# Identity products in TensorE's gaps until the first FFN product, and V sorting of batch 0 through three PSUM banks

## The chip, the cores and the metric

The kernel runs on one core of a Trainium2 chip. The metric is device microseconds of one execution; the runs shown are given by their median. The profile is of one further execution, recorded by the hardware profiler. Times within it count from the start of its span.

The core has a matrix engine (TensorE, "PE" in the profile, with weight loads as "PEld"), VectorE ("DVE"), ScalarE ("ACT"), GpSimd ("POOL") and SyncE ("SP"), each working through its own list of instructions in order. Matrix products land in PSUM, which the kernel uses as eight banks of 512 f32 columns. Transfers are issued by GpSimd and SyncE and run on 16 DMA engines.

## The reference

Two stages in a row. First block-sorted attention for 4 batches, 8 heads, 768 positions in 8 blocks of 96, head size 64:

```
P = sort_net                        # [4, 8, 8, 8]
five times: P = exp(P - rowmax); P /= rowsum; P /= columnsum
k_sorted = einsum('bhij,bhjcd->bhicd', P, k_blocks)      # blocks mixed by P
v_sorted = einsum('bhij,bhjcd->bhicd', P, v_blocks)
scores   = q_block @ k_sorted_block.T / 8                 # block by block, 96 x 96
attn     = softmax(scores)
x        = attn @ v_sorted_block                          # [3072 tokens, 512]
```

Then a feed-forward network (FFN): `h = x @ w_in` (512 to 2048), `g = max(h, 0) + alpha * min(h, 0)`, `out = g @ w_out` (2048 to 512), in f32.

## The kernel before, in words

**Groups and stages.** Attention works on 32 groups g (batch g // 8, block g % 8), each with all 8 heads. Before a batch's groups, its K and V are sorted. K sorting of a batch is six units (`prep_k`, products of line 542), V sorting eight units (`prep_v`, products of line 585). Each unit is 16 small products into one PSUM bank and one copy out of it (line 372, `copy`), by ScalarE or VectorE. V is first copied into another layout (`conv_v`, tile VD from VST). The matrices of the sorting weights, BDK, come from the Sinkhorn steps on VectorE and ScalarE (`sinkhorn`, `spread`).

**A group of batch 0** is: scores (line 625, `s1`), row maxima on VectorE (line 631), scores once more transposed and with the maxima taken off by identity products (lines 646 and 637, `s2`), exp on ScalarE (line 669, tile Es), product with sorted V (line 678, `o`), reciprocal and scaling on VectorE (lines 683 and 686, tile xq), transpose on TensorE (line 701), and copy to xT. A group of a later batch takes its maxima off inside the exp (line 658) and is transposed by DMA (lines 663 and 694, tiles ET and xT). Groups 0 and 1 run side by side: group 0 uses psS and psO, group 1 uses psH for scores and psYP for its output.

**The FFN** takes chunks of 2 or 4 groups of tokens. `ffn1` is four products of line 723 into a bank, a ReLU of the negated bank on ScalarE (line 733, tile t) and a combination on VectorE that reads the bank again (line 736, tile hT). `ffn2` is four parts of four products each (line 762) and a copy out.

**PSUM banks.** psS, psO, psH and psYP have two banks each. `BANK_O` are the banks of psO, `BANK_H` those of psH, `BANK_Y` is bank 0 of psYP and `BANK_P` its bank 1. While `ffn1` works on the first two groups it also uses `BANK_P`; the sorting of batch 1 goes through `BANK_P` alone. V sorting of batch 0 goes through both banks of psO, `BANK_P` and `BANK_Y` in turn (line 795).

**The order of the work** isn't written out. Every piece is an operation in a graph (`_Graph`) with an estimated duration, a priority and the tiles that it reads and writes. `schedule` plays the graph through with these estimates and puts each engine's operations in order; for operations that may run on ScalarE or VectorE it also picks the engine. `search` does so 1500 times with priorities changed at random (a fixed seed) and keeps the order with the lowest estimated end. The result is a fixed list for each engine, with semaphore waits. A change in the graph changes the search, and so the order of the whole kernel.

**Filling.** After the search, `fill` goes through TensorE's list. Where the estimates leave a gap inside one of the given spans of time, it puts a block of identity products into it that nobody reads: as many as take 0.9 of the gap. They write `BANK_Y`, 512 columns each (`warm`, line 877). There are two spans: from 5 us to the first V sorting unit that uses `BANK_Y`, and from the first `ffn1` product to the first `ffn2` product.

**Loads.** GpSimd issues all loads of q, k, v and the weights: q, k and v of batch 0, the four parts of w_in, the two of w_out, k of batch 1 (line 419), q of batch 1 in eight parts (line 401), then v of batch 1 and k and v of batch 2 (line 419). `ffn1` needs w_in, `ffn2` needs the halves of w_out, K sorting of batch 1 needs KS and its V layout copies need VST.

Of the kernel before, what the change touches and what calls it, by code (L numbers as in the profile page):

```python
# [8 lines left out]
AP = bass.AP  # L9
# [26 lines left out]
def t_pe(*mms):  # L36
    return sum(max(n, m, 64) / 2.4 + 4 for n, m in mms)


def t_act(n):  # L40
    return 170 + n / 1.2
# [19 lines left out]
class _Graph:  # L61
# [138 lines left out]
            op.prio = p  # L200
        return self.schedule()

    def fill(self, make, unit, first, spans):

        out, last = [], self.ops[first].end + 300
        for op in self.order["pe"]:
            for lo, hi in spans:
                begin = max(last, lo)
                n = int((op.start - begin) * 0.9 / unit)
                if op.start <= hi and n > 0:  # L210
                    x = _Op("pe", lambda e, n=n: make(e, n), n * unit, 0.0, None, len(self.ops))
                    x.start, x.end = begin, begin + n * unit
                    x.deps.add(first)
                    self.ops.append(x)
                    out.append(x)
            out.append(op)
            last = max(last, op.end)
        for pos, op in enumerate(out):
            op.pos = pos
        self.order["pe"] = out  # L220
# [69 lines left out]
def bass_sinkhorn_attn__then__act_prelu_kernel(  # L290
# [11 lines left out]
    G = _Graph()  # L302
    sems = {e: es.enter_context(nc.semaphore("s_" + e)) for e in ENGS}

    def dma_sem(name):
        return [es.enter_context(nc.semaphore("d_" + name)), 0]
# [7 lines left out]
    PE, ACT, DVE, POOL, SYNC = ("pe",), ("act",), ("dve",), ("pool",), ("sync",)  # L314
# [251 lines left out]
                                               AP(KT[0], 0, [[ld, 128], [bk, 32], [1, 16]])), 900,  # L566
                  r=[("KT", 0, 0), ("KT", 0, 1)], w=["KTpad"], prio=prio + 1)

    first_y = []

    def conv_v(b, u, prio):
        o = AP(VD, 8 * u * 64, [[4096, 128], [64, 8], [1, 48]])
        i = AP(VST[b % 2], 8 * u, [[3072, 128], [1, 8], [64, 48]])
# [3 lines left out]
    def prep_v(b, u, prio, bank=BANK_P):  # L577
        t, off, row, keys = bank
        n = b % 2

        def f(e):
            inst = None
            for dd in range(8):
                for th in range(2):
                    inst = e.matmul(AP(t, th * 64 * row + off + dd * 64, [[row, 64], [1, 64]]),  # L585
                                    AP(VD, (8 * u + dd) * 64, [[4096, 128], [1, 64]]),
                                    AP(BDK, b * 128 + th, [[512, 128], [2, 64]]))
            return inst
        op = G.add(PE, f, 374, r=[("VD", u), "VD0", ("BDK", b)], w=keys, prio=prio)
        if keys == ["psY"]:  # L590
            first_y.append(op)
        o = AP(VS[n], 8 * u, [[64 * 65, 112], [65, 64], [1, 8]])
        i = AP(t, off, [[row, 112], [1, 64], [64, 8]])
        G.add(EITHER, lambda e: copy(e, o, i), {"act": 685, "dve": 690}, r=keys + [("VS1", n)], w=[("VS", n, u)],
              prio=prio)

    d_e = [dma_sem("e%d" % n) for n in range(NE)]
    d_x = [dma_sem("x%d" % n) for n in range(NE)]

    def attention(g, prio):  # L600
# [53 lines left out]
        if far:  # L654
            def ex(e):
                inst = None
                for p in range(8):
                    inst = e.activation(AP(Esb[me], p * 128, [[1024, 96], [64, 2], [1, 48]]),  # L658
                                        AP(psX, (p // 4) * 512 + (p % 4) * 96, [[1024, 96], [48, 2], [1, 48]]),
                                        ACTF.Exp, bias=nf[m][:, p:p + 1])  # L660
                return inst
            G.add(ACT, ex, 8 * 245, r=banks_s + [("Epad", me), ("nf", m)], w=[("Esb", me)], prio=prio)
            G.add(SYNC, lambda e: e.dma_start_transpose(
                AP(ET[me], 0, [[800, 128], [96, 8], [1, 96]]), AP(Esb[me], 0, [[1024, 96], [1, 1024]])),
                5000 if g < 18 else 3100, r=[("Esb", me)], w=[("ET", me), ("turned", g)], prio=prio, dma=(d_e[me], 0))
        else:
            G.add(PE, s2, 700, r=kt_keys + qt_keys + [("nm", m), "identb"],
                  w=banks_s, prio=ps_)
            G.add(ACT, lambda e: e.activation(
                AP(Es0[m], 0, [[800, nk], [384, 2], [1, 384]]),  # L670
                AP(psX, 0, [[1024, nk], [512, 2], [1, 384]]),
                ACTF.Exp), t_act(768), r=banks_s, w=[("Es0", m)], prio=ps_)

        def o(e):
            inst = None
# [3 lines left out]
                                    AP(ET[me] if far else Es0[m], pos(h4, hp) * 96, [[800, nk], [1, 128]]),  # L679
                                    AP(VS[n], ((hp * 4 + h4) * 8 + i) * 65, [[64 * 65, nk], [1, 65]]))  # L680
            return inst
        G.add(PE, o, t_pe(*[(65, 65)] * 8), r=vs_keys + ([("ET", me), ("ETtail", me)] if far else [("Es0", m), ("Etail", m)]), w=banks_o, prio=prio)
        G.add(DVE, lambda e: e.reciprocal(AP(rec[m], 0, [[8, 96], [4, 2], [1, 4]]),  # L683
                                          AP(psZ, 64, [[1024, 96], [512, 2], [68, 4]])), 200,
              r=banks_o, w=[("rec", m)], prio=prio)
# [106 lines left out]
    for u in range(8):  # L792
        conv_v(0, u, -45.5)
    for u in range(8):
        prep_v(0, u, -45, (BANK_O + [BANK_P, BANK_Y])[u % 4])
    for kt in range(KT_TILES):
        G.add(POOL, lambda e, kt=kt: e.dma_start(
            AP(w_in_bf, kt * DFF, [[KT_TILES * DFF, 128], [1, DFF]]),
# [72 lines left out]
    assert fp == len(ffn_plan)  # L871
    total = G.search(SEARCH)

    def warm(e, n):
        inst = None
        for _ in range(n):
            inst = e.matmul(psYP[:, 0, :], identb[:, :], AP(identb, 0, [[128, 128], [0, 4], [1, 128]]))  # L877
        return inst
    G.fill(warm, 215, ident_op, [(5000, first_y[0].start), (ffn_ops[0].start + 1, ffn_ops[1].start)])
    if __import__("os").environ.get("SCHED"):  # L880
        print("scheduled", total)
        for e in ENGS:
# [37 lines left out]
```

## Time and profile before

| | |
|---|---|
| runs shown | 253.9, 254.17, 256.3 us; median 254.17 |
| the profiled execution | 255.69 us, its span 254.0 us |
| TensorE busy | 235.3 us (93%) |
| VectorE, ScalarE, GpSimd busy | 171.5, 160.5, 38.5 us |
| identity products of line 877 | 34, 10.6 us |
| first FFN product | 27.61 us |
| first K and V sorting of batch 1 on TensorE | 42.03 and 52.09 us |

In the page's table of slices each digit is one fortieth of the span, 6.35 us, and gives the busy share in tenths; 9 is 90% or more. PEclk is the clock granted to TensorE in tenths of full speed. In the chain of work that ended last, the FFN products of lines 723 and 762 have 29% and 26 + 3% of the span. A timeline row gives start, duration, engine, line, operation, output and inputs, shape and count, and in brackets the idle time before it and what ended it.

### The profile page before, as it was taken

What the parts mean: (1) busy time and instruction counts of PE and PEld (TensorE: products, weight loads), DVE (VectorE), ACT (ScalarE), POOL (GpSimd) and SP (SyncE); (2) the same over time, 40 slices, a digit from 0 to 9 for tenths busy, and PEclk for the clock granted to TensorE, in tenths of its full rate; (3) what the DMA queues carried; (4) which work ended last, traced back from release to release, by engine and by line L of the source; (5) the groups of instructions that cost most, each with busy time, mean ns of one, the idle gap of its engine ahead of it and who ended that gap; (6) DMA issues with size and microseconds to landing.
All of it is one profiled execution on the core that took longest, in us unless ns stands there. A gap on an engine that the chain in (4) does not pass through costs nothing.

```text
span 254.0 us, 6423 instructions
## 1 busy us (share of the span) xinstructions
PE 235.3 (93%) x2679; PEld 140.7 (55%) x2679; DVE 171.5 (68%) x347; ACT 160.5 (63%) x429; POOL 38.5 (15%) x63
## 2 busy tenths in 40 slices
PE   4796899989997978989899999999999999999995
PEld 1455678657654544556555555555555555555554
DVE  5887668796856775977885666656667765645530
ACT  4475446598866765878866485766677457534531
POOL 8995000000360011037000000000000000000000
PEclk9999589999999999999999999999999999999999
DMA  5999999999999999999979345233234433311103
GB/s 102 211 211 203 181 215 166 216 188 187 101 159 106 172 162 143 220 146 183 94 158 149 67 115 130 50 90 85 71 70 122 80 66 88 90 58 40 43 5 122
DMA packets 75534, 32.17 MB, mean 127 GB/s; under 512 B 67808, under 2 KB 71152, under 8 KB 75504
## 3 DMA queue, kind: packets, MB, share of 16 engines
q0 software_dynamic: 23632, 13.63, 41.1%
q1 hardware_dynamic: 51872, 18.11, 38.7%
q8 instruction: 21, 0.34, 0.6%
q14 instruction: 9, 0.07, 0.1%
HBM read 27.28 MB, written 6.29 MB: 132 GB/s over the span
## 4 chain that ended last, share of the span: by engine, by line
PE 75%; DVE 12%; DMA 9%; ACT 2%; issue 1%
PE psH L723 29%; PE psYP L762 26%; DMA ET<-Esb 8%; PE psS L762 3%; PE psO L678 3%; PE psS L622 3%; PE psYP L585 3%; PE psYP L542 2%; DVE hT L736 2%; DVE VD L372 2%; DVE VS L372 1%; PE psYP L877 1%; PE psS L637 1%; DVE KT L372 1%; ACT Esb L658 1%
## 5 line engine op out<-in xcount | busy, mean ns | idle before, releaser
L736 DVE SCALAR_TENSOR_TENSOR hT<-t,omaT,psH 128x384 bf16<-128x384 f32 (+1 forms) x139 | 77.5, 572 | 39.7 <-ACT t L733 38.1
L723 PE MATMUL psH<-xT,w_in_bf 128*128 128x384 bf16 (+1 forms) x556 | 98.5, 314 | 1.6 <-DVE hT L736 1.3
L733 ACT ACTIVATE t<-psH 128x384 f32<-128x384 f32 (+1 forms) x139 | 62.8, 466 | 44.5 <-PE psH L723 41.4
L762 PE MATMUL psYP<-w_out_bf,hT 128*128 128x512 bf16 x336 | 83.9, 379 | 1.0 <-DVE hT L736 0.6
L723 PEld LDWEIGHTS psH<-xT,w_in_bf 128*128 128x128 bf16 x556 | 50.8, 99 | 35.0 <-DVE hT L736 7.8
L658 ACT ACTIVATE Esb<-psS,nf 96x96 bf16<-96x96 f32 x192 | 46.3, 345 | 2.1 <-DVE nf L631 2.1
L762 PEld LDWEIGHTS psYP<-w_out_bf,hT 128*128 128x128 bf16 x336 | 30.7, 98 | 29.7 <-DVE hT L736 0.7
L401 POOL DMA_DIRECT2D QN<-in_q_dram x24 | 20.0, 857 | 45.2 <-DMA QTz<-QN 44.5
L631 DVE TENSOR_REDUCE nf<-psS 96x8 f32<-96x768 f32 x24 | 22.7, 948 | 3.9 <-PE psS L622 3.9
L686 DVE TENSOR_TENSOR xq<-psO,rec 96x512 bf16<-96x512 f32 x31 | 21.3, 686 | 1.0
L372 ACT ACTIVATE VS<-psYP 112x512 bf16<-112x512 f32 x17 | 11.7, 689 | 6.3 <-PE psYP L585 6.2
L372 ACT ACTIVATE outstg<-psYP 128x512 f32<-128x512 f32 x15 | 9.0, 597 | 9.9 <-PE psYP L762 9.8
L585 PE MATMUL psYP<-BDK,VD 128*64 128x64 bf16 x448 | 12.4, 198 | 1.9 <-DVE hT L736 1.0
L683 DVE RECIPROCAL rec<-psO 96x8 f32<-96x8 f32 x31 | 6.2, 201 | 11.7 <-PE psO L678 11.7
L877 PE MATMUL psYP<-identb 128*128 128x512 bf16 x34 | 10.6, 451 | 3.4 <-ACT identb L372 3.4
L585 PEld LDWEIGHTS psYP<-BDK,VD 128*64 128x64 bf16 x448 | 9.3, 111 | 6.9 <-issue 1.8
L622 PEld LDWEIGHTS psS<-KT,QTz 128*96 128x96 bf16 x192 | 11.7, 124 | 2.5
L678 PEld LDWEIGHTS psO<-VS,ET 112*128 112x128 bf16 x192 | 8.6, 98 | 7.6 <-DMA ET<-Esb 4.4
L622 PE MATMUL psS<-KT,QTz 128*96 128x96 bf16 x192 | 12.7, 209 | 0.0
L678 PE MATMUL psO<-VS,ET 112*128 112x65 bf16 x192 | 9.9, 194 | 2.8 <-DMA ET<-Esb 2.6
L372 DVE COPY VD<-VST 128x384 bf16<-128x384 bf16 x20 | 10.5, 565 | 1.4 <-DMA VST<-in_v_dram 1.4
L372 ACT ACTIVATE KT<-psYP 128x512 bf16<-128x512 f32 x11 | 6.6, 600 | 6.7 <-PE psYP L542 6.5
(115 smaller groups left out, 174.6 us busy)
## 6 DMA issues: line engine op xcount, KB each, us to landing
out_dram<-outstg SPq DMA_DIRECT2D x23, 256.0 KB, 2.2
KS<-in_k_dram POOLq DMA_DIRECT2D x3, 768.0 KB, 33.4
VST<-in_v_dram POOLq DMA_DIRECT2D x3, 768.0 KB, 29.1
QN<-in_q_dram POOLq DMA_DIRECT2D x24, 96.0 KB, 5.9
w_in_bf<-in_moe_w_in_dram POOLq DMA_DIRECT2D x4, 512.0 KB, 17.7
w_out_bf<-in_moe_w_out_dram POOLq DMA_DIRECT2D x2, 1024.0 KB, 28.4
QS<-in_q_dram POOLq DMA_DIRECT2D x1, 768.0 KB, 6.6
VST<-in_v_dram POOLq DMA_DIRECT2D x4, 192.0 KB, 4.6
```

Source lines behind the costliest of these rows:

```text
L372: return e.activation(o, i, ACTF.Copy) if e is nc.scalar else e.tensor_copy(o, i)
L401: G.add(POOL, lambda e, h=h: e.dma_start(AP(QN, h * 128 + (h // 4) * 64, [[6144, 128], [1024, 6], [1, 64]]), AP(q.tensor, b * HB + h * S * ...
L585: inst = e.matmul(AP(t, th * 64 * row + off + dd * 64, [[row, 64], [1, 64]]), AP(VD, (8 * u + dd) * 64, [[4096, 128], [1, 64]]), AP(BDK, b ...
L622: inst = e.matmul(o, AP(QTz[n], hp * 3072 + h4 * 768 + i * 96, [[6144, 128], [1, 96]]), AP(KT[n], (h4 * 8 + i) * bk, [[ld, 128], [64, 2], ...
L631: G.add(DVE, lambda e: e.tensor_reduce(AP(nx, 0, [[8, 96], [4, 2], [1, 4]]), AP(psX, 0, [[1024, 96], [512, 2], [96, 4], [1, 96]]), AxisLis ...
L658: inst = e.activation(AP(Esb[me], p * 128, [[1024, 96], [64, 2], [1, 48]]), AP(psX, (p // 4) * 512 + (p % 4) * 96, [[1024, 96], [48, 2], [ ...
L678: inst = e.matmul(AP(psZ, hp * 512 + h4 * 68, [[1024, 128], [1, 65]]), AP(ET[me] if far else Es0[m], pos(h4, hp) * 96, [[800, nk], [1, 128]]),
L686: G.add(DVE, lambda e: e.tensor_tensor(out=AP(xq[me], 0, [[512, 96], [256, 2], [64, 4], [1, 64]]), in0=AP(psZ, 0, [[1024, 96], [512, 2], [ ...
L723: inst = e.matmul(AP(pt, poff, [[1024, 128], [1, n]]), AP(w_in_bf, kt * DFF + ft * 128, [[KT_TILES * DFF, 128], [1, 128]]), AP(xT, kt * XR ...
L733: G.add(ACT, lambda e: e.activation(AP(t1[tb], 0, [[384, 128], [1, n]]), AP(pt, poff, [[1024, 128], [1, n]]), ACTF.Relu, scale=-1.0), t_ac ...
L736: G.add(DVE, lambda e: e.scalar_tensor_tensor(out=AP(hT, ft * RING + tok % RING, [[FT_TILES * RING, 128], [1, n]]), in0=AP(t1[tb], 0, [[38 ...
L762: inst = e.matmul(AP(bank[0], bank[1], [[1024, 128], [1, n]]), AP(hT, ft * RING + tok % RING, [[FT_TILES * RING, 128], [1, 128]]), AP(w_ou ...
```

## The change

The spans given to `fill` now carry what a block of identity products must wait for and the bank that it writes. There are three: from 5 us to group 1's output product, into `BANK_Y`, after the identity matrix is made; from there to the first `ffn1` product, into the first bank of psH, after group 1's exp, the last reader of its scores there; and from there to the first `ffn2` product, into `BANK_Y` again. An identity product now has 256 columns with an estimate of 108 ns, in place of 512 and 215. So that `BANK_Y` is free of V sorting until group 1's output, the V sorting of batch 0 takes three banks in turn, both of psO and `BANK_P`.

```diff
@@ class _Graph
-    def fill(self, make, unit, first, spans):
-
-        out, last = [], self.ops[first].end + 300
+    def fill(self, make, unit, spans):
+
+        out, last = [], 0.0
         for op in self.order["pe"]:
-            for lo, hi in spans:
-                begin = max(last, lo)
+            for lo, hi, deps, bank in spans:
+                begin = max([last, lo] + [self.ops[d].end + 300 for d in deps])
                 n = int((op.start - begin) * 0.9 / unit)
                 if op.start <= hi and n > 0:
-                    x = _Op("pe", lambda e, n=n: make(e, n), n * unit, 0.0, None, len(self.ops))
+                    x = _Op("pe", lambda e, n=n, bank=bank: make(e, n, bank), n * unit, 0.0, None, len(self.ops))
                     x.start, x.end = begin, begin + n * unit
-                    x.deps.add(first)
+                    x.deps.update(deps)
                     self.ops.append(x)
                     out.append(x)
             out.append(op)
...
@@ prep_v
-        op = G.add(PE, f, 374, r=[("VD", u), "VD0", ("BDK", b)], w=keys, prio=prio)
-        if keys == ["psY"]:
-            first_y.append(op)
+        G.add(PE, f, 374, r=[("VD", u), "VD0", ("BDK", b)], w=keys, prio=prio)
...
@@ attention: group 1's exp and output product are noted
+            if g == 1:
+                warm_at["exp"] = op
...
+        if g == 1:
+            warm_at["out"] = op
...
     for u in range(8):
-        prep_v(0, u, -45, (BANK_O + [BANK_P, BANK_Y])[u % 4])
+        prep_v(0, u, -45, (BANK_O + [BANK_P])[u % 3])
...
-    def warm(e, n):
+    def warm(e, n, bank):
+        t, off, row, keys = bank
         inst = None
         for _ in range(n):
-            inst = e.matmul(psYP[:, 0, :], identb[:, :], AP(identb, 0, [[128, 128], [0, 4], [1, 128]]))
+            inst = e.matmul(AP(t, off, [[row, 128], [1, 256]]), identb[:, :], AP(identb, 0, [[128, 128], [0, 2], [1, 128]]))
         return inst
-    G.fill(warm, 215, ident_op, [(5000, first_y[0].start), (ffn_ops[0].start + 1, ffn_ops[1].start)])
+    out1, f1, f2 = warm_at["out"].start, ffn_ops[0].start, ffn_ops[1].start
+    G.fill(warm, 108, [(5000, out1, [ident_op], BANK_Y), (out1 + 1, f1, [warm_at["exp"].idx], BANK_H[0]),
+                       (f1 + 1, f2, [ident_op], BANK_Y)])
```

In the built order there are 87 identity products ahead of the first FFN product (29 of twice the width before) and 12 between the first FFN product and the first product of line 762 (5 before). Since the bank turn of V sorting enters the graph, the search gives another order, from the K sorting of batch 0 to the end of the kernel.

## The prediction

> **What bounds the kernel now.** I read the page's 40 slices first, then the clock by its own windows, then TensorE's timeline from 20 to 60 us, then when the loads land. In the slices TensorE (PE) is near full from 28 us on. The clock row has one dip, and the DMA row is full until slice 20 (127 us).
>
> ```profile
> PE   4796899989997978989899999999999999999995
> PEclk9999589999999999999999999999999999999999
> DMA  5999999999999999999979345233234433311103
> ```
>
> The dip, cut into stretches of 3.41 us (a row: stretch, its length, busy time and count of TensorE, granted clock, DMA share, GB/s):
>
> ```profile
> 19.83:23.24 3.41, 2.59 (x101) 1.00 1.07 215
> 23.24:26.65 3.41, 1.50 (x28) 1.00 1.03 156
> 26.65:30.06 3.41, 3.26 (x39) 0.50 1.20 194
> 30.06:33.47 3.41, 3.41 (x25) 0.50 1.24 207
> ...
> 9.60:13.00 3.40, 1.90 (x16) 1.00 0.99 204
> ```
>
> After a stretch that was 44% busy (1.50 of 3.41) the clock is halved for 6.82 us, though no single gap in that stretch exceeds 0.77 us. A stretch 56% busy (9.60 to 13.00) did not halve it. So the share of a stretch seems to decide, with the limit between 44 and 56%.
>
> What the dip costs: from the first FFN product (27.61 us) to 33.47 us TensorE did work that takes about 3.1 us at full clock (sums of the same groups in later rows: 0.66 for 8 FFN products of 192 columns, 0.28 + 0.36 for the second score pass, 0.65 for three identity products, and so on). It took 5.8 us, so 2.7 us are lost. Will the end get them? Two later places decide:
>
> ```profile
> 27.61 1.46 PE L723 MATMUL psH<-xT,w_in_bf 128*128 128x192 bf16 x8
> ...
> 42.03 0.44 PE L542 MATMUL psYP<-BDK,KS 64*64 64x64 bf16 x16
> ```
>
> ```profile
> 52.09 0.44 PE L585 MATMUL psYP<-BDK,VD 128*64 128x64 bf16 x16 [0.97 <-DVE hT L736]
> ```
>
> These are the first K sorting and the first V sorting of batch 1. Their data comes from these loads (start of issue on GpSimd, then time from issue to landing):
>
> ```profile
> 8.17 0.62 POOL L419 DMA_DIRECT2D KS<-in_k_dram  x1
> ...
> 21.16 1.14 POOL L419 DMA_DIRECT2D VST<-in_v_dram  x2
> ```
>
> ```profile
> KS<-in_k_dram POOLq DMA_DIRECT2D x1, 768.0 KB, 33.4
> ```
>
> ```profile
> VST<-in_v_dram POOLq DMA_DIRECT2D x1, 768.0 KB, 29.1
> ```
>
> K of batch 1 lands at 8.17 + 33.4 = 41.57, 0.46 us before its use at 42.03. V lands at 21.16 + 29.1 = 50.26, and VectorE and ScalarE start on it at 50.32. Between them lie 8 Q loads, the last landing at 46.6. The loads are one queue on DMA engines that are full (share 1.0 to 1.2) from 6 us on, so these are fixed dates. Today TensorE arrives at both without slack: **the start is bound by loads as much as by the clock**.
>
> **The change, part by part.**
>
> *Fill and clock.* The built order has 87 identity products of 256 columns ahead of the first FFN product (29 of 512 before) and 12 behind it (5). In the stretch that ended in the dip there are now blocks of 7, 7, 5 and 2. At 0.109 us each (0.2155 us, the spacing of 512 columns in the 0.86 us rows of four, halved) they add 2.3 us to 1.50 of 3.41. The dip at 26.65 us goes: -2.7 us if nothing else binds. Below nothing: a block stands ahead of a real product and may delay it, by 2.3 us in all if every product were ready already. I take 0.0, because the products behind them wait for the output chain on VectorE (reciprocal 0.20, product 0.69, twice), which the blocks don't enter.
>
> *Three banks for V sorting of batch 0.* A bank is held for 0.44 us of products and a copy of 0.69, with hand-over some 1.3 us. Three banks give 2.3 units per us, two copying engines at 0.62 to 0.69 us give 3. Only the last four of eight units run back to back: 4/2.3 - 4/3 = 0.4 us later. Against it, the new order puts the last K copy of batch 0 on VectorE directly after two others, so the first scores start near 16.7 us instead of 17.39. Walking the new order by the old rows, I get the last V copy near 24.1 us and the first FFN product near 27.5 (27.61). Bounds: 0.7 earlier (but w_in's last part lands at 5.93 + 20.6 = 26.53) to 1 us later. I take 0. Cover: the K date, with some 1.8 us of slack, as follows.
>
> *What is late next.* The planner's search ran anew, so all later order differs, but I counted the work: between the first FFN product and the first V sorting of batch 1 both orders hold the same products but for fill (18.4 and 18.6 us at full clock), and 187 us behind it in both. From the first FFN product to the first K sorting the new order has 11.6 us of work. Today's full-clock part (33.5 to 42.03, 8.5 us for 8.0 of work) gives a factor 1.06, so 27.5 + 12.3 = 39.8 us. There TensorE must wait for K until 41.6, 1.8 us, and as it works in order nothing passes. Of 2.7 us at most 0.4 survive. The K stretch then holds 7.1 us of work through a single PSUM bank (six rounds of 0.44 + 0.07 + 0.69 = 7.2), so it ends near 49.4 us, and V lands at 50.26.
>
> Then the order around V matters. Today:
>
> ```profile
> 50.32 0.86 ACT L372 ACTIVATE VD<-VST 128x384 bf16<-128x384 bf16 x1
> 51.16 0.33 ACT L733 ACTIVATE t<-psYP 128x192 f32<-128x192 f32 x1
> ```
>
> ```profile
> 50.32 1.40 DVE L372 COPY VD<-VST 128x384 bf16<-128x384 bf16 x3
> 51.62 0.41 DVE L736 SCALAR_TENSOR_TENSOR hT<-t,omaT,psYP 128x192 bf16<-128x192 f32 x1
> ```
>
> The V product needs the bank of an FFN product, which ScalarE (t) and then VectorE (hT) must read first: hence 52.09. In the new order ScalarE has copy of V, copy of xT, copy of V, and only then that t. At spacings of 0.78, 0.40, 0.78 and 0.30 us from 50.32, t ends at 52.6, hT at 53.0, and the V product starts at 53.05: **0.95 us later than today**, with the same work behind it.
>
> *The clock again.* TensorE then idles from about 49.4 to 53.05 us, 3.6 us. However the grid of 3.41 us stretches lies, one holds at least 1.8 us of it; on today's grid that is 50.5 to 53.9 with about 0.9 busy (26%). By the two rows above that halves the clock, near 53.9. If the spell lasts 6.82 us as today's, it costs 6.82 x 2.7/5.8 = 3.2 us, less 0.3 us for which TensorE idles today in that stage (7.76 of 8 busy from 54 to 62): 2.9.
>
> The Trainium skill, "TensorE: Matmul & The Clock Gate", section "Why this matters for your kernels", says to avoid TensorE gaps of over about 3 us, as one idle window brings the half clock back. Today's dip came with gaps of at most 0.77 us, so the trace speaks for a share rather than a gap. By the page the 1.8 us at K couldn't cool the clock and the 3.6 us at V would; by the share both may.
>
> *The rest of the order.* The two traces' late parts can't be told apart by counting. The end has 2.6 us of TensorE waits for the transposed scores (ET); they could all go or double, so +-2.6 us. I take 0.
>
> **Sum.** Dip gone -2.7, taken back at the dates of K and V +2.7, V chain +0.95, new half-clock spell +2.9: +3.85 us. The profiled execution took 255.69 us (span 254.0 and 1.7 around it); it would be 259.5. It lies 1.5 above the median of the runs, 254.17, which with the same sum becomes **258.0**.
>
> **Rivals.**
> - *No new spell.* The wait at K (1.8 us, at least 56% busy unless one stretch holds it whole) cools the clock instead, and the slow K stretch fills the idle time before V; or the idle time at V falls evenly on two stretches. Then only +0.95: 255.1. For it: the limit is known only to lie between 44 and 56%.
> - *The gain is kept (not slower).* If V landed by 47.6 us instead of 50.26, or the new order hid the wait, the 2.7 us come through: 251.5. It decides at K landing before 39.8 and V before 47.6. For it speaks only that today neither wait shows; against it the fixed spacing of the landings (41.6, 46.6, 50.3).
> - *The change misses its aim:* the dip at 26.65 stays. Then TensorE arrives at V as today and only the V chain remains: 255.1. Against it: 1.50 + 2.3 of 3.41 busy.
>
> **How the numbers follow.** New spell 0.46, no new spell 0.31, gain kept 0.17, dip stays 0.06. The likeliest gives 258.0; a spell of one stretch instead of two, or the ET waits, move it by some 2 us. The range 252.0 to 260.0 leaves out two thirds of the third case (0.11) and the top of the first (0.05). A difference of 1% (2.5 us) is about what a measurement of this kernel can tell from none: its runs spread over 253.9 to 256.3. Faster by more: most of the kept gain and a little of the second case, 0.14. Slower by more: 0.39 of the first case and 0.07 of the others, 0.46. Within: 0.40. The forecast's own case spans 256 to 260.
>
> **What would show it.** In the new profile: full clock from 26 to 33 us; the first FFN product at 27 to 28; a TensorE wait of 1 to 2 us ending at 41.6 at K; the V copies starting at 50.3 and the first V product near 53; a half clock somewhere in 50 to 61. Wrong if K or V land much earlier than 41.6 and 50.3, if the clock stays full through 61 us, or if the late part loses or gains more than 2.6 us.

## The result, and the profile after

The changed kernel took **256.89 us** (median of 20 runs, 254.69 to 260.26), the kernel before beside it 254.86 us (20 runs, 252.36 to 257.44). The ratio is 1.0079, 95% interval 1.0049 to 1.0108: some 2 us slower, within the 1% that the prediction takes as no difference. The forecast was 258.0 with a range of 252.0 to 260.0. The number was near; the working behind it was right in half of its steps only, and this is what the rest is about.

The profiled execution took 259.17 us (span 257.5), one of the longest of its kernel, so what it shows is taken as the kernel's only where a second profile (run 8 below, 255.53 us, span 253.8) or the other runs of the same order show it too; the ratios, and the means below, leave out executions over 1.5% above the fastest of their kernel.

The table of slices after the change, as before: busy tenths of TensorE, its granted clock, and the DMA engines' share.

```profile
PE   4799999789898889989899999999899999999995
PEclk9999999979999999999999999999999999999999
DMA  5999999999999999999957245333333235202022
```

The dip in the fifth and sixth slices of the clock row is gone in this execution; a shorter one stands in the ninth. The same by stretches of the clock, TensorE's busy time first (columns: stretch, its length, then busy time and count of TensorE, its weight loads, VectorE, ScalarE and GpSimd, granted clock, DMA share, GB/s):

```profile
26.55:29.97 3.42, 3.07 (x43) 2.00 (x42) 2.16 (x4) 1.51 (x4) 0.00 (x0) 1.00 1.21 193
29.97:33.38 3.41, 3.41 (x52) 2.70 (x51) 2.95 (x9) 2.02 (x6) 0.00 (x0) 1.00 1.26 211
...
50.45:53.86 3.41, 1.11 (x20) 0.64 (x20) 2.15 (x7) 3.39 (x8) 0.00 (x0) 0.99 1.04 212
53.86:57.27 3.41, 3.41 (x56) 2.56 (x55) 2.65 (x8) 1.86 (x6) 0.00 (x0) 0.51 1.11 165
```

From 26.6 to 33.4 us the clock is full, where it was half. After a stretch with 1.11 of 3.41 us busy it is halved at 53.86 us, for one stretch of 3.41 us. The two landmarks of the prediction and the first FFN product, in TensorE's timeline:

```profile
28.91 0.82 PE L724 MATMUL psH<-xT,w_in_bf 128*128 128x192 bf16 x8
...
41.34 0.44 PE L542 MATMUL psYP<-BDK,KS 64*64 64x64 bf16 x16
...
52.75 0.44 PE L583 MATMUL psYP<-BDK,VD 128*64 128x64 bf16 x16 [2.50 <-DVE hT L737]
```

The first FFN product comes 1.3 us later than before (27.61), the first K sorting of batch 1 stands behind no wait, and the first V sorting of batch 1 comes 0.66 us later (52.09), after an idle time of 2.50 us instead of 0.97. What holds the V product is seen on ScalarE and VectorE:

```profile
50.06 0.85 ACT L372 ACTIVATE VD<-VST 128x384 bf16<-128x384 bf16 x1 [1.86 <-DMA VST<-in_v_dram]
...
51.92 0.32 ACT L734 ACTIVATE t<-psYP 128x192 f32<-128x192 f32 x1
```

```profile
52.28 0.42 DVE L737 SCALAR_TENSOR_TENSOR hT<-t,omaT,psYP 128x192 bf16<-128x192 f32 x1 [1.26 <-ACT t L734]
```

ScalarE waits 1.86 us for V to land, copies, and reads the FFN bank (t) only at 51.92 us; before, that read stood at 51.16. The product follows hT.

### The granted clock of every execution

Each execution comes with the mean clock granted to TensorE. A stretch of 3.41 us at half clock takes 0.5 x 3.41 / 254 = 0.0067 off the mean. The view of the two profiles of the changed kernel:

```profile
core 0: 257.5 us, clock 0.993
```

```profile
core 0: 253.8 us, clock 1.000
```

One stretch in the first, none in the second, as their traces have it; in all 14 profiles of this study the number worked out so agrees with the spells in the trace (those within the span). So the half-clock stretches can be counted in the executions without a trace too, and their times compared. The count doesn't say where in the execution they lie. Mean time in us by number of half-clock stretches (number of executions; the single executions of runs 8 and 12 are counted with their kernels):

| kernel | none | 1 | 2 | 3 |
|---|---|---|---|---|
| before | | 254.42 (20) | 254.25 (55) | 255.02 (6) |
| changed | 256.44 (3) | 256.19 (10) | 257.14 (5) | |
| fill alone (run 1) | 253.05 (5) | 253.58 (2) | 255.53 (1) | 256.10 (1) |
| order and banks alone (run 2) | | | 255.92 (5) | 257.00 (4) |
| before, V product delayed (run 9) | | 253.05 (5) | 254.30 (4) | 254.77 (3) |

One more execution of run 2, with four stretches, took 258.06 us. Two readings carry what follows. In the kernel before, one stretch and two give the same time (254.42 and 254.25; 253.8 and 254.2 beside runs 1 to 8, 255.3 and 254.3 on the other chip, beside runs 9 to 12): the second stretch of the dip is not seen at the end. What the first one costs this row can't say, since no execution before is without it. And the changed kernel without any half-clock stretch takes 256.4 us, 2.0 us more than the kernel before with one: **the clock is not where the changed kernel loses**.

### The profile page after: what moved, and what is told of

The parts are those of the page before. It is cut to its first block, busy times and chain, and to the rows that moved or that the text cites. A ratio compares the mean times of both kernels' runs of the same rounds, so it can differ in the third digit from the quotient of the medians.

```text
span 257.5 us, 6567 instructions
## 1 busy us (share of the span) xinstructions
PE 237.3 (92%) x2744; PEld 145.7 (57%) x2744; DVE 176.7 (69%) x354; ACT 156.0 (61%) x422; POOL 40.1 (16%) x63
## 4 chain that ended last, share of the span: by engine, by line
PE 63%; DMA 24%; DVE 5%; ACT 4%; POOL 2%; issue 1%
PE psH L724 26%; PE psYP L763 23%; DMA VST<-in_v_dram 11%; DMA ET<-Esb 9%; PE psS L763 3%; DMA xT<-xq 3%; PE psO L677 3%; PE psS L619 2%; PE psYP L583 2%; POOL QN L401 2%; ACT Esb L655 1%; PE psYP L542 1%; ACT t L734 1%; DVE hT L737 1%; PE psO L763 1%
## 5 line engine op out<-in xcount | busy, mean ns | idle before, releaser
L724 PE MATMUL psH<-xT,w_in_bf 128*128 128x384 bf16 (+1 forms) x556 | 97.1, 312 | 1.9 <-DVE hT L737 1.3
L763 PE MATMUL psYP<-w_out_bf,hT 128*128 128x512 bf16 x336 | 84.9, 380 | 0.1
L724 PEld LDWEIGHTS psH<-xT,w_in_bf 128*128 128x128 bf16 x556 | 49.9, 98 | 34.7 <-DVE hT L737 6.5
L401 POOL DMA_DIRECT2D QN<-in_q_dram x24 | 21.7, 927 | 49.6 <-DMA QTz<-QN 49.6
L879 PE MATMUL psYP<-identb 128*128 128x256 bf16 x85 | 12.6, 295 | 3.4 <-ACT identb L372 3.4
L684 DVE RECIPROCAL rec<-psO 96x8 f32<-96x8 f32 x31 | 6.2, 200 | 12.5 <-PE psO L677 12.3
L372 ACT ACTIVATE outstg<-psYP 128x512 f32<-128x512 f32 x13 | 7.8, 597 | 8.6 <-PE psYP L763 8.6
L372 ACT ACTIVATE VD<-VST 128x384 bf16<-128x384 bf16 x13 | 10.5, 859 | 2.2 <-DMA VST<-in_v_dram 2.2
L372 ACT ACTIVATE VS<-psYP 112x512 bf16<-112x512 f32 x13 | 8.9, 688 | 4.3 <-PE psYP L583 4.2
L372 DVE CAST KT<-psYP 128x512 bf16<-128x512 f32 x12 | 8.2, 687 | 4.2 <-PE psYP L542 4.1
```

Source lines behind the costliest of these rows:

```text
L372: return e.activation(o, i, ACTF.Copy) if e is nc.scalar else e.tensor_copy(o, i)
L401: G.add(POOL, lambda e, h=h: e.dma_start(AP(QN, h * 128 + (h // 4) * 64, [[6144, 128], [1024, 6], [1, 64]]), AP(q.tensor, b * HB + h * S * ...
L724: inst = e.matmul(AP(pt, poff, [[1024, 128], [1, n]]), AP(w_in_bf, kt * DFF + ft * 128, [[KT_TILES * DFF, 128], [1, 128]]), AP(xT, kt * XR ...
L763: inst = e.matmul(AP(bank[0], bank[1], [[1024, 128], [1, n]]), AP(hT, ft * RING + tok % RING, [[FT_TILES * RING, 128], [1, 128]]), AP(w_ou ...
```

## The experiments

Runs 1 to 4, 5 to 8 and 9 to 12 were each timed beside the kernel before (254.47, 254.13 and 254.85 us), the first eight on one chip and the last four on another. "First FFN product" and "V product" (the first V sorting of batch 1) are from the profile of the run.

### 1. Fill alone

The order and the four banks of before; only the new fill, its first span ending where V sorting first takes `BANK_Y`. All other instructions stand as before.

```diff
-    G.fill(warm, 215, ident_op, [(5000, first_y[0].start), (ffn_ops[0].start + 1, ffn_ops[1].start)])
+    G.fill(warm, 108, [(5000, first_y[0].start, [ident_op], BANK_Y),
+                       (out1 + 1, f1, [warm_at["exp"].idx], BANK_H[0]), (f1 + 1, f2, [ident_op], BANK_Y)])
```

> The order and the four banks of the kernel before, with the new identity products wherever a bank is free (not during the second half of V sorting of batch 0). Theory (the dates at which K and V of batch 1 land take the gain back): the half clock after 26.7 us goes, the first FFN product stays near 27.6 us, TensorE waits some 2 us ahead of the first V sorting of batch 1, which starts near 52 us as before; time 254.4 to 256.4 us, the upper end if that wait halves the clock again. Rival (the order found by the new search costs the time, not the loads): 2 to 2.7 us faster than the kernel before, 252 to 253 us.

Measured: 253.76 us (252.51 to 259.91), ratio 0.9957, interval 0.9909 to 1.0005. First FFN product 27.48 us, no early dip. TensorE's timeline, two rows of this run:

```profile
41.36 0.44 PE L542 MATMUL psYP<-BDK,KS 64*64 64x64 bf16 x16 [1.68 <-DMA KS<-in_k_dram]
...
107.12 0.60 PE L681 MATMUL psO<-VS,ET 112*128 112x65 bf16 x8 [5.37 <-DMA ET<-Esb]
```

The first row is the wait at K that the prediction forecast at 1.8 us: 1.68 us of what the dip gave back is spent waiting for a load. The V product stays at 51.88 us (52.09). The second row explains this run's long profile (257.6 us span): a wait of 5.37 us for a transposed score, from 101.75 us, and two stretches at half clock that begin 3.4 us into it, at 105.19 us. The time lies between the two expectations (254.4 to 256.4, and 252 to 253): of the dip's 2.7 us some 1.1 are kept by the ratio (between none and 2.3 by its interval), and the larger part is taken back. The fill by itself makes the kernel no slower; if anything it gains 0.4%.

### 2. Order and banks alone

The changed kernel's graph, so its order and its three banks, with the fill of before (512 columns, in the time up to the fourth V unit and between the first FFN products).

```diff
-    G.fill(warm, 108, [(5000, out1, [ident_op], BANK_Y), (out1 + 1, f1, [warm_at["exp"].idx], BANK_H[0]),
-                       (f1 + 1, f2, [ident_op], BANK_Y)])
+    G.fill(warm, 215, ident_op, [(5000, first_y[3].start), (ffn_ops[0].start + 1, ffn_ops[1].start)])
```

> The order and the three banks of the changed kernel, with the identity products of the kernel before (512 columns, only up to the fourth V unit of batch 0 and between the first two FFN stages). Theory: the half clock after 26 us is back, TensorE comes to the V sorting of batch 1 late enough that its wait there is under 1.5 us, no half clock in 50 to 61 us; first V product at 52.7 us; some 0.7 us slower than before, 255.5 us. Rival (the new order loses in its late part): as slow as the changed kernel or slower, 256.9 to 258 us.

Measured: 256.83 us (254.91 to 260.11), ratio 1.0072, interval 1.0028 to 1.0116. That is the rival's time, and the whole slowdown of the changed kernel (1.0079) with no new fill in it. First FFN product 28.43 us, V product 52.60. The stretches around its two spells:

```profile
21.90:25.31 3.41, 1.91 (x67) 1.59 (x66) 1.42 (x4) 1.42 (x3) 1.47 (x3) 1.00 1.08 198
25.31:28.72 3.41, 2.17 (x27) 1.37 (x24) 2.30 (x5) 0.98 (x2) 0.00 (x0) 0.50 1.12 164
...
49.20:52.62 3.42, 2.06 (x45) 1.40 (x42) 2.97 (x7) 3.10 (x6) 0.00 (x0) 1.00 1.06 217
52.62:56.03 3.41, 3.41 (x40) 1.87 (x41) 1.97 (x5) 2.02 (x5) 0.00 (x0) 0.50 1.07 200
```

The clock is halved after 1.91 of 3.41 us busy (56%), and again after 2.06 of 3.42 (60%). The early dip and the one at V both occur here. With two stretches this kernel takes 255.92 us, the kernel before with two 254.25 (254.30 on the same chip, beside this run).

### 3. The wait at V filled

The changed kernel with 20 identity products of 256 columns into the second bank of psO ahead of the V product, so that the idle time there cannot cool the clock.

```diff
+    x = _Op("pe", lambda e: warm(e, 20, BANK_O[1]), 1.0, 0.0, None, len(G.ops))
+    x.deps.update(d for d in warm_at["out6"].deps if d in G.reads_of["psO1"])
+    pe.insert(pe.index(warm_at["v1"]), x)
```

> The changed kernel with 20 more identity products (some 2.2 us) in TensorE's wait ahead of the first V sorting of batch 1, into a bank of psO that is free then. Theory: the half clock near 54 us goes, the first V product stays at 52.7 us, and 1.5 us come back: 255.4 us. Rival (the half clock there costs nothing, since other engines bind): unchanged, 256.9 us.

Measured: 257.89 us (255.36 to 261.63), ratio 1.0133, interval 1.0092 to 1.0174. Counted as in the table above, its executions have no half-clock stretch (257.35 (3)) or one (257.46 (7)), and in its profile there is none near V; the one it has lies from 24.49 to 27.90 us, although its list for TensorE is that of the changed kernel up to V. It is still the slowest of all. In the profile TensorE came to the place late, and the block itself held the V product back:

```profile
52.41 2.35 PE L909 MATMUL psO<-identb 128*128 128x256 bf16 x20
...
54.69 0.44 PE L609 MATMUL psYP<-BDK,VD 128*64 128x64 bf16 x16
```

So removing the spell behind V, priced at 2.9 us, returned nothing that could be seen, but the run added a delay as well and doesn't price the spell alone. A V product 1.5 to 1.9 us later than in the two profiles of the changed kernel stands beside a time 0.5% longer by the ratios (1.0133 against 1.0079); their intervals overlap, so that this delay was paid for is likely and not certain.

### 4. V of batch 1 loaded earlier

The changed kernel with the load of V moved ahead of the eight loads of Q on GpSimd's queue (issued at 13.59 instead of 22.23 us).

```diff
+    pool.remove(vload)
+    pool.insert(pool.index(first_q), vload)
```

> The changed kernel with the load of V of batch 1 issued ahead of the eight Q loads of batch 1 instead of behind them; nothing else moves. Theory: V lands near 45 to 46.5 us, TensorE no longer waits 2.5 us for it, no half clock follows: 4 us come back, 252.9 us, faster than the kernel before. Rival 1 (a later stage takes it back, the score transposes or the Q transposes, which now start some 4 us later): 255 to 257 us. Rival 2 (the landing isn't set by the queue's order): unchanged.

Measured: 256.15 us (254.16 to 259.73), ratio 1.0043, interval 1.0003 to 1.0082. The wait for V on ScalarE is gone, but in this profile TensorE came late itself (half clock from 23.15 to 29.98 us, first FFN product 31.81 us), so that the V product came at 54.01 us, later than in the changed kernel, after an idle time of 0.87 us for hT.

By the ratios a gain of 0.4% over the changed kernel, with intervals that overlap. The 4 us of the theory didn't come back; that the landing of V is a part of the price stays possible, since this profile doesn't show the earlier V used.

### 5 and 6. Wider and narrower identity products

The changed kernel with the same columns of identity products in half as many instructions (512 wide), and in twice as many (128 wide).

```diff
-        for _ in range(n):                                  # 256 columns each
+        for w in [512] * (n // 2) + [256] * (n % 2):        # run 5
+        for _ in range(2 * n):                              # run 6, 128 columns each
```

> The changed kernel, with each pair of identity products of 256 columns as one of 512: the same columns in the same places, 42 products fewer ahead of the first FFN product. Theory 2 (TensorE's own instructions arrive in pieces of some 127 products, and it stands still at the 223rd and 350th product until the next piece is there): the 350th product is now two V units later, the stand-still in V sorting shrinks, the first FFN product is 0.5 us or more earlier than in the changed kernel on the average, and the time is 256.2 us or less. Rival (the number of instructions is nothing to the time): 256.9 us, the stand-still at the same V unit.

> The changed kernel, with each identity product of 256 columns as two of 128: the same columns, 87 more products ahead of the first FFN product. Theory 2 (pieces of instructions): the 350th product now falls before the first V unit, TensorE stands still there and once more in V sorting, the first FFN product is at 30 us or later, and the time is 258 us or more. Rival: 256.9 us.

Measured: 257.12 us (255.13 to 262.05), ratio 1.0078, interval 1.0037 to 1.0118, with 512 columns; 257.28 us (255.82 to 259.0), ratio 1.0116, interval 1.0082 to 1.0150, with 128. Between 47 and 174 identity products ahead of the first FFN product the time moves by 0.4%, within the intervals; the times of theory 2 (256.2 or less, 258 or more) both failed. The early part is late in both profiles: the first FFN product came at 30.08 and 32.84 us. Two things stand ahead of it, a standstill for which the profile names no releaser ("issue"), and half clock behind that, in run 5 from 24.31 to 27.72 us and in run 6 from 21.28 to 28.11. The standstill in run 6:

```profile
21.24 0.47 PE L643 MATMUL psS<-QTz,KT 64*128 64x96 bf16 x7 [2.21 <-issue]
```

More on it under the hardware. A first FFN product 2.8 us later (32.84 against 30.08) is seen in the end time with at most a small part.

### 7. Fill alone, V loaded earlier

Run 1 with the edit of run 4.

> The order and banks of the kernel before with the new identity products where a bank is free, as in the first experiment, and the load of V of batch 1 ahead of the eight Q loads. Theory (the date of V takes the gain of the full clock): the wait ahead of the first V sorting of batch 1 (1.44 us in the first experiment) goes, and the time is 252.3 us, faster than the kernel before by 0.8%. Rival (a later stage takes it back): 253.8 us as in the first experiment.

Measured: 254.7 us (252.64 to 259.61), ratio 0.9974, interval 0.9938 to 1.0010. K wait 1.83 us, V product at 51.97 us after 0.87 us, now for hT alone. The earlier V brings the old order nothing: with V landed, the chain through t and hT sets the same date.

### 8. The changed kernel again

> The changed kernel once more, for a second profile. If the stand-still in V sorting differs from execution to execution: the first FFN product between 28.5 and 32 us, a half-clock spell either in 21 to 30 us or behind 50 us. If the first profile is typical: first FFN product at 28.9 us, first V sorting of batch 1 at 52.75 us, half clock near 54 us.

Measured, one execution: 255.53 us, span 253.8. Three rows of TensorE's timeline:

```profile
22.32 0.48 PE L583 MATMUL psO<-BDK,VD 128*64 128x64 bf16 x19 [1.34 <-issue]
...
29.75 0.24 PE L702 MATMUL psYP<-identb,xq 96*128 96x96 bf16 x2 [1.43 <-issue]
...
53.19 0.44 PE L583 MATMUL psYP<-BDK,VD 128*64 128x64 bf16 x16 [1.07 <-DVE hT L737]
```

With the standstills the first FFN product came at 30.79 us, and so TensorE reached V late, idled only 1.07 us there, and the clock stayed full throughout. A kernel whose order is fixed has its spell at V in one execution and not in the next, depending on when TensorE gets there.

### 9. The V product delayed in the kernel before

Run 3's block of 20 identity products in the kernel before; nothing else changed. This asks whether the date of the V product is what is paid for.

> The kernel before, with 20 identity products of 256 columns (2.2 us at full clock) into the second bank of psO directly ahead of the first V product of batch 1, which stood at 52.09 us after a wait of 0.97 us. Order, banks and fill are otherwise those of before. It asks whether the date of that V product alone is the price. Theory (the new order is slower because its first V product comes some 1.2 us later): the V product moves to about 53.3 us and the whole to about 255.5 us, +1.2 us over before on the same chip (ratio 1.0047), what the changed kernel pays of its 2.0 us. Rival (slack behind it takes the delay, and the price of the new order lies elsewhere): the V product moves and the time stays within 0.3 us of before, about 254.4.

Measured: 254.0 us (252.41 to 255.42), ratio 0.9965, interval 0.9934 to 0.9996. The V product came **3.2 us later** than before, and the kernel was not slower:

```profile
52.55 2.81 PE L914 MATMUL psO<-identb 128*128 128x256 bf16 x20
55.28 0.44 PE L612 MATMUL psYP<-BDK,VD 128*64 128x64 bf16 x16
```

The theory that the new order is slower because of its later V product falls, at least for the old order. What took the delay up is seen in TensorE's waits behind the V product, first in the kernel before (columns: engine, operation and line, waited for, us in total, times, longest):

```profile
PE psO L678 <- DMA ET<-Esb: 2.6, 3, 1.3
PE psH L723 <- DVE hT L736: 1.3, 4, 0.7
```

and then in run 9, where no wait for the transposed scores (ET) is left:

```profile
PE psYP L793 <- issue: 1.1, 7, 0.2
PE psYP L793 <- DVE hT L767: 0.8, 1, 0.8
PE psH L754 <- DVE hT L767: 0.5, 3, 0.2
```

In the kernel before these waits stand at 80.03 (1.28 us), 92.23 (0.69) and 110.51 us (0.68); in its second profile (run 12) they make 2.1 us. A TensorE that comes later waits less there, which accounts for some 2 to 2.6 of the 3.2 us; the rest isn't traced.

### 10. ScalarE's read of the FFN bank first

The changed kernel with ScalarE's t from psYP moved ahead of its first copy of V.

```diff
+    act.remove(tee)
+    act.insert(act.index(first_v), tee)
```

> The changed kernel, with ScalarE's read of the FFN bank (tile t from psYP, line 734) moved ahead of its first copy of V of batch 1; nothing else moves. Theory (the chain behind the landing of V, copy, copy, copy, t, hT, sets the first V product at 52.75 us): t no longer waits for V, hT ends by about 51 us, and the V product starts when the first copy of V is done, near 51.2 us, 1 to 1.5 us earlier, where TensorE is there by then; the time falls by 0.5 to 1.2 us to 255.7 to 256.4. Rival (TensorE gets to V about as late as the chain, since its first FFN product is late): V product at 52.3 or later, time unchanged within 0.4 us of 256.9.

Measured: 256.66 us (254.35 to 259.11), ratio 1.0071, interval 1.0033 to 1.0109: the rival, no change. In its profile TensorE is late again (first FFN product 31.15 us), so t waits for TensorE, and the copy of V behind it; the V product then waits 1.25 us for that copy and starts at 53.73 us:

```profile
52.52 0.33 ACT L763 ACTIVATE t<-psYP 128x192 f32<-128x192 f32 x1 [2.08 <-PE psYP L753]
52.74 0.84 ACT L396 ACTIVATE VD<-VST 128x384 bf16<-128x384 bf16 x1
```

Moving t put one date in the place of another, so this run doesn't say what a shorter chain is worth.

### 11. Fill alone, K and V loaded earlier

Run 7, with K of batch 1 also moved ahead of w_out's second half.

```diff
+    pool.remove(kload)
+    pool.insert(pool.index(w_outs[1]), kload)
```

> The old order with the new fill (as in the run of fill alone), with K of batch 1 loaded ahead of w_out's second half and V of batch 1 ahead of the eight parts of Q. Theory (loads are fixed dates, and the wait of 1.7 to 1.8 us at K is where the gain of the fill goes): K lands 3 to 4 us earlier, the wait at K is gone, the first V product comes at about 50.3 us instead of 51.9, and the time is 252.3 to 253.0, ratio 0.993 to 0.996 to before. Rival (something else, as w_out's second half or the later dates of Q and of batch 2, takes the place): the wait at K is gone but the time stays at 254.2 to 254.7.

Measured: 254.28 us (252.26 to 259.1), ratio 0.9963, interval 0.9923 to 1.0003. The wait at K is gone, but in the profile TensorE was late through a half-clock spell from 22.61 to 29.44 us (first FFN product 30.62, first K product 42.75 with no wait), so the profile doesn't show an early K used. The interval holds both the theory's upper end and the rival; inconclusive. Its three executions without half clock took 252.33 us on average, 0.7 under the five of run 1, on another chip, and 2.0 under the kernel before with two stretches on its own chip (254.31). That is what the theory asks for, but in three executions picked by their clock: an early K may be worth it, and the run doesn't show it.

### 12. The kernel before again

> The kernel before once more, for a second profile of it. If its dates repeat: first FFN product 27.3 to 27.9 us, first V product of batch 1 at 51.9 to 52.2 us, a half-clock spell of 3.4 or 6.8 us within 22 to 36 us. If the changed kernel's spread of 28.4 to 32.8 us of the first FFN product is a spread of the chip and not of its order, this one shows a date past 28.5 us.

Measured, one execution: 253.83 us, span 252.1; first FFN product 27.73 us, V product 52.07, half clock from 26.05 to 32.87 us. The dates of the kernel before repeat within 0.15 us, against 28.91 and 30.79 us for the first FFN product in two profiles of the changed one. So the later and wandering date goes with the changed kernel, as far as two profiles of each can say. Two variants of the old order with the new fill have 27.48 and 27.99 us (runs 1 and 7), the third 30.62 behind a half-clock spell (run 11).

## Why the prediction was right, and where it wasn't

The sum was -2.7 (dip) + 2.7 (taken back at K and V) + 0.95 (V chain) + 2.9 (new spell) + 0 (late order) = +3.85 us; measured +2.0. The time itself was nearer, 258.0 against 256.89, in part by luck: the sum stood on 254.17 us, and the kernel before took 254.86 beside the changed one.

**Dip gone, and taken back: right in the main.** The profile of the fill alone has no early dip, waits 1.68 us at K as forecast (1.8), and the time changes by -0.4% with an interval (0.9909 to 1.0005) that touches none; so the larger part of the 2.7 us is taken back; how much is kept is open (1.1 us by the ratio, where the prediction had at most 0.4). But the fill doesn't always hold the clock: of the eight profiles with 256 columns three have an early half-clock spell (runs 3, 4 and 11, from 24.49, 23.15 and 22.61 us), where all four with the fill of before have one. In the changed kernel itself the wait at K did not show: from the first FFN product to K it needed 12.4 us (forecast 12.3), but it came to K at 41.34 us, not at 39.8, because it was late already.

**Three banks, "I take 0", first FFN product 27.5 us: wrong.** It came at 28.43 (run 2), 28.91 and 30.79 us, in the two profiles of the changed kernel outside the bound of "1 us later". The working followed the banks' hand-over and the engines, but not the standstills of TensorE at 21 to 23 and 28 to 30 us. The first of them stands in the kernel before too, ahead of the 351st product as in the changed kernel, where the profile puts it down to a copy that had ended 0.5 us before:

```profile
22.32 0.45 PE L585 MATMUL psYP<-BDK,VD 128*64 128x64 bf16 x16 [0.82 <-DVE VS L372]
```

The second stands ahead of the 478th product. In the kernel before the first FFN product is the 435th and so lies ahead of that count; in the changed kernel it is the 493rd. How much of the 0.8 to 3.2 us is the three banks' own was not separated. The step did little harm: what follows hides much of it.

**V chain +0.95: right in its date (52.75 against 53.05), wrong in its price.** The date held although TensorE reached V at 50.25 us, not at 49.4 (and 41.6 + 7.2 is 48.8), because the chain behind V's landing set it. In the kernel before a V product 3.2 us later costs nothing (run 9), mostly because the waits for the transposed scores give the time back. In the changed order a delay of 1.5 to 1.9 us may have been paid with 0.5% (run 3, which was not timed side by side with the changed kernel), so there its price stays open between nothing and most of it.

**New half-clock spell, 2.9 us: there in the first profile, of half the length, and not what is paid.** It was assumed to last two stretches, as the old dip; of 18 executions 5 have two stretches, 10 one and 3 none, wherever they lie (run 3 and run 4 had theirs before 30 us). Two cost 0.95 us more than one (257.14 against 256.19), one no more than none (256.19 against 256.44). The term was oversized by 2 us or more. The rule it stood on, a busy share between 44 and 56%, fell too: the clock cooled after 60% (run 2, 49.20 to 52.62 us) and 66% (run 7, 48.32 to 51.73 us), and not after 46% in this row of run 5, followed by full clock:

```profile
51.62:55.03 3.41, 1.58 (x36) 1.00 (x38) 2.20 (x6) 3.39 (x8) 0.00 (x0) 1.00 1.05 198
```

The Trainium skill, "TensorE: Matmul & The Clock Gate", section "Why this matters for your kernels", puts it on idle windows of about 3 us. The 5.37 us wait of run 1, with half clock from 3.4 us into it, agrees; the spell of the changed kernel, whose longest wait there was 2.50 us, and the dip of before with none over 0.77 us in the stretch ahead of it don't. What decides is open.

**The rest of the order, "+-2.6, I take 0": the term that failed.** With order and banks alone the kernel has the whole slowdown (1.0072). At an equal number of half-clock stretches it is 1.7 and 2.0 us slower than before (255.92 against 254.25 with two, 257.00 against 255.02 with three), the changed kernel 1.8 and 2.9 (256.19 against 254.42 with one, 257.14 against 254.25 with two). So some 2 us of the new order and its banks, which no run separates, were counted as nothing, and a spell that costs under 1 us as 2.9: two errors that nearly cancel, and a forecast within 0.5% that was only partly earned.

**Where in the order the 2 us lie** is not settled. A pointer: in all eight profiles of the new order, TensorE stands twice behind the V product where none of the six of the old order has such a wait, here in the first profile of the changed kernel:

```profile
65.89 0.28 PE L583 MATMUL psYP<-BDK,VD 128*64 128x64 bf16 x6 [0.50 <-ACT VS L372]
...
70.86 0.82 PE L724 MATMUL psH<-xT,w_in_bf 128*128 128x384 bf16 x4 [0.53 <-DVE hT L737]
```

Together 1.0 us, a chain of bank, copy and product that the search built in the new order. TensorE's idle time as a whole doesn't tell the orders apart: from the V product to the end it is 10.8 and 10.7 us in the two profiles of the changed kernel and 8.5 and 9.6 in the two of before, but 8.0 in run 2, which is as slow as the changed kernel, and over all profiles 6.6 to 11.0 in the new order and 7.5 to 10.8 in the old. Two profiles whose V products lie close, with no half clock behind them, point the same way as the two waits: run 9, in the old order, needs 197.2 us from 55.28 us to the end, run 6, in the new one, 199.8 from 55.04. No run took the waits out, and single profiles of one kernel differ by 2 us in that part; it is argued, not shown.

**Of the rivals**, "no new spell" (255.1) describes run 8's profile, but not its cause; "the gain is kept" fell with the K wait of run 1. The range held the time; a time within 1% had the second largest chance, 0.40 against 0.46 for slower.

## What to carry to other kernels

Where loads land at fixed dates, a clock dip ahead of them may cost little, and filling it buys a wait; look for the next fixed date before pricing a dip, and for the one behind it before pricing a delay. When an edit to a planned order makes the planner search anew, price the new order by a run with everything else put back: here order and banks were the whole difference, while the fill, the edit's own subject, was free. The mean granted clock of each execution can be turned into a count of half-clock stretches, which separates the clock's share of a time from the order's without a trace.

## What the runs showed of the hardware

**TensorE stops at fixed counts of instructions.** Most of TensorE's early standstills without a named releaser lie behind the same number of products, whatever these are: at the 223rd (run 10, 15.85 us, 0.51 us), the 350th (0.53 us in the changed kernel at 21.52, 1.34 in run 8 at 22.32, 2.21 in run 6 at 21.24) and the 477th (1.43 us in run 8 at 29.75). They are 127 products apart, each with a weight load. A queue of the DMA table fits them, in the changed kernel (packets, MB, share of 16 engines):

```profile
q8 instruction: 21, 0.34, 0.5%
```

21 packets of some 16 KB: it seems that the program itself comes in pieces, on DMA engines that are full until 127 us, and that TensorE stands when it has used up a piece before the next is there. In all eight profiles of the new order the stop behind the 350th product ends between 21.2 and 22.8 us, although run 6 got there with twice the identity products and run 5 with half of them. The times of these packets in the traces fit too: in all 14 profiles, the old order's among them, the second packet ended 1.25 to 1.53 us before the 351st product began, whether TensorE had idled 0.2 us there or 2.2 us, and where TensorE stood ahead of the 478th, it began 1.36 to 1.44 us after the third packet's end. So that TensorE waits for a piece is likely; no run moved a packet by itself, and what holds the packets back is open. A block of filler makes the count run ahead.

**A spell of half clock lasts one stretch of 3.41 us or two** (6.83), on a grid that starts differently in each execution, so that the same kernel has from none to three of them (run 1 in the table of clocks). How busy the stretch ahead was does not decide by itself: stretches that were 33 to 66% busy cooled, one of 46% and one of 55% (run 5 from 51.62 us, the changed kernel from 9.48) did not.
